# Strassen's second product and another token order for the read-out rows of a fused cross-attention and feed-forward kernel

## The chip, the cores and the metric

The kernel runs on one core of one Trainium2 chip. The metric is the device time of one execution in microseconds. The time before is the median of 13 executions.

## The reference, cut to what matters

There are 8 batches and 8 heads, 512 tokens and 32 state rows for each head, 64 values wide. Attention goes both ways, and the two results are put one behind the other, so that each batch has 512 + 32 = 544 rows of 512 values. A feed-forward stage with exact GELU and d_ff = 2048 follows.

```python
a = softmax(scale * x @ state.T);   xread = a @ state      # 512 rows for each head
a2 = softmax(scale * state @ x.T);  sread = a2 @ x         # 32 rows for each head: the read-out
x = concat([xread, sread], axis=2)  # heads side by side: 8 * 544 rows of 512
h = x @ w_in                        # w_in: 512 x 2048
g = 0.5 * h * (1 + erf(h / sqrt(2)))
out = g @ w_out                     # w_out: 2048 x 512
```

The change concerns the 8 * 32 = 256 read-out rows. Their rows in the output lie at b*544 + 512 to b*544 + 543, for batch b.

## The kernel before, in words

The order of all instructions is written out by hand; each engine takes its instructions in that order. Matrix products have bf16 operands and fp32 sums.

**Token rows.** For a batch, `M` runs the first product in 16 pieces m of 128 hidden values. Each is two matmuls of 512 columns (L478) into a PSUM bank, followed by the GELU on ScalarE (L485), which writes `g`. The second product runs for batches 2 to 7 by Strassen's seven products: `X(b, name)` is one of them, 16 matmuls of 256 columns (L602). VectorE forms the sums of quadrants of `g` that the products need (`g_sum`, L596), sums of quadrants of `w_out` are formed once (`w_sums`), and the products are added up by ScalarE (copies out of PSUM), GpSimd (L621, L650: it forms `v` and `u`) and VectorE (L624, L645, L656, L658).

**Slots.** The last loop goes over batches b = 2 to 7 and eight slots p = 0 to 7. A slot holds two pieces of `M(b)`, one product of batch b - 1 or b, and smaller work. Products 4, 5, 1, 2 and 7 of batch b - 1 run in slots 0 to 4, products 3 and 6 of batch b in slots 6 and 7. Product 2 ends with `c22`: GpSimd forms `v` (L621), then VectorE adds it to the sixth product (L624), then SyncE issues the transfer of half the batch.

**Read-out rows.** `sread` in slot 1 computes a batch's read-out, `sread_out` scales it into `srm`. `srt` transposes `srm` on TensorE (L402), and VectorE copies the result from PSUM to `XSR` (L405), at the columns of that batch, b*32 to b*32 + 31. It stands late in slot 3, after product 2 of the batch before and its `c22`. When `XSR` holds all eight batches, `mm1_sr(m)` runs a piece of the first product for all 256 read-out rows: 4 matmuls of 256 columns (L519) and a GELU of 128x256 (L526) into `g_sr`. Sixteen pieces are needed; four run in each of the slots 4 to 7 of the last batch, between `M` and the product of that slot. The second product, `mm2_sr(s)`, is 16 matmuls of 512 columns for each half s of the rows (L531), a VectorE copy (L539) and an output transfer (L540).

**The end.** After the loop come, for the last batch, the products 4, 5, 1, 2 and 7, with `mm2_sr(0)` after product 4 and `mm2_sr(1)` ahead of product 7. Product 7 is cut in two halves; each ends with a VectorE addition (L678) and a transfer of 128x256 values (L682), the first issued by SyncE, the last by ScalarE.

**Buffers.** Four PSUM banks (the pool `ps_f`) serve the pieces `hp` and `hps`, `srT` and the results of `mm2_sr`. Four more hold the products (`otile`).

Of the kernel before, what the change touches and what calls it, by code (L numbers as in the profile page):

```python
# [9 lines left out]
FP32 = mybir.dt.float32  # L10
BF16 = mybir.dt.bfloat16
AF = mybir.ActivationFunctionType
ALU = mybir.AluOpType
# [4 lines left out]
def kernel(  # L18
# [20 lines left out]
    persist = ctx.enter_context(tc.tile_pool(name="persist", bufs=1))  # L39
    xin = ctx.enter_context(tc.tile_pool(name="xin", bufs=2))  # L40
    att = ctx.enter_context(tc.tile_pool(name="att", bufs=2))
    gpool = ctx.enter_context(tc.tile_pool(name="gpool", bufs=2))
    opool = ctx.enter_context(tc.tile_pool(name="opool", bufs=4))
    hpool = ctx.enter_context(tc.tile_pool(name="hpool", bufs=1))
    apool = ctx.enter_context(tc.tile_pool(name="apool", bufs=3))
    cpool = ctx.enter_context(tc.tile_pool(name="cpool", bufs=1))
    PSUM = bass.MemoryType.PSUM
    ps_f = ctx.enter_context(tc.tile_pool(name="ps_f", bufs=4, space=PSUM))
# [6 lines left out]
    def otile(shape, name, at=None):  # L55
        if at is None:
            at = turn[0] % 4
            turn[0] += 1
        return ps_o.tile(shape, FP32, name=name, tag=f"o{at}")

    def ftile(shape, name):
        return ps_f.tile(shape, FP32, name=name, tag="f")
# [4 lines left out]
    w_out_bf = persist.tile([128, MC, d_model], BF16, name="w_out_bf")  # L67
    ident = persist.tile([128, 128], BF16, name="ident")
    sbd = persist.tile([128, B, HC, 2 * NS], BF16, name="sbd")
    XSR = persist.tile([128, HC, B * NS], BF16, name="XSR")  # L70
    g_sr = persist.tile([128, MC, B * NS], BF16, name="g_sr")
    st_f = persist.tile([128, 2, D], FP32, name="st_f")
    st_bf = persist.tile([128, B, 2, D], BF16, name="st_bf")
# [290 lines left out]
    def atr_dma(b):  # L364
        A = atts[b]
        A.AT = att.tile([128, SJ, 2, 128], BF16, name="AT", tag="AT")
        nc.sync.dma_start_transpose(
            out=A.AT.rearrange("p j t n -> p (j t) n"), in_=A.a
        )
# [29 lines left out]
    def srt(b):  # L399
        A = atts[b]  # L400
        ps = ps_f.tile([128, HC, NS], BF16, name="srT", tag="f")
        nc.tensor.transpose(  # L402
            ps.rearrange("p c n -> p (c n)"), A.srm.rearrange("q t d -> q (t d)"), ident
        )
        nc.vector.tensor_copy(out=XSR[:, :, b * NS:(b + 1) * NS], in_=ps)  # L405

    Ps = {}

# [78 lines left out]
    ops = {}  # L487
# [28 lines left out]
    def mm1_sr(m):  # L516
        hp = ps_f.tile([128, B * NS], FP32, name="hps", tag="f")
        for c in range(HC):
            nc.tensor.matmul(  # L519
                hp,  # L520
                lhsT=w_in_bf[:, c, m * 128:(m + 1) * 128],
                rhs=XSR[:, c, :],
                start=(c == 0),
                stop=(c == HC - 1),
            )
        nc.scalar.activation(out=g_sr[:, m, :], in_=hp, func=AF.Gelu)  # L526

    def mm2_sr(s):
        ps = ps_f.tile([128, d_model], FP32, name="ops", tag="f")
        for m in range(MC):  # L530
            nc.tensor.matmul(  # L531
                ps,
                lhsT=g_sr[:, m, s * 128:(s + 1) * 128],
                rhs=w_out_bf[:, m, :],
                start=(m == 0),
                stop=(m == MC - 1),
            )
        osb = opool.tile([128, d_model], FP32, name="osb", tag="osb")
        nc.vector.tensor_copy(out=osb, in_=ps)  # L539
        nc.sync.dma_start(  # L540
            out=out.rearrange("(b s) n -> b s n", s=SB)[4 * s:4 * s + 4, S:SB, :], in_=osb
        )


    def mm2_m(b, m):
        for j in range(SJ):
# [11 lines left out]
    MH = MC // 2  # L558
    NH = d_model // 2
    w_q = [[w_out_bf[:, MH * k:MH * k + MH, NH * n:NH * n + NH] for n in range(2)] for k in range(2)]  # L560
    w_sum = {}
# [18 lines left out]
        )[i])  # L580

    xs = {}

    def g_q(b, h, k):
        return gs[b][:, MH * k:MH * k + MH, 256 * h:256 * h + 256]

    def g_sum(b, name):
        (h0, k0), (h1, k1), op = {
            "1": ((0, 0), (1, 1), ALU.add),
            "2": ((1, 0), (1, 1), ALU.add),  # L590
            "5": ((0, 0), (0, 1), ALU.add),
            "6": ((1, 0), (0, 0), ALU.subtract),
            "7": ((0, 1), (1, 1), ALU.subtract),
        }[name]
        t = apool.tile([128, MH, 256], BF16, name="gsum", tag="gsum")
        nc.vector.tensor_tensor(out=t, in0=g_q(b, h0, k0), in1=g_q(b, h1, k1), op=op)  # L596
        xs[b, "g" + name] = t
# [13 lines left out]
    def c_tile(name):  # L611
        return cpool.tile([128, 2, NH], FP32, name=name, tag=name)
# [50 lines left out]
    def X1_split(b):  # L663
        xs[b, "q"] = c_tile("q")
        for j in range(2):
            ps = xs[b, "x", j] = otile([128, 1, NH], "xp", 2 - 2 * j)
            x_mm(ps, xs[b, "g1"], w_sum["1"], True, (j,))
            nc.vector.tensor_tensor(
                out=xs[b, "q"][:, j, :], in0=ps[:, 0, :], in1=xs[b, "s34"][:, j, :], op=ALU.add
            )  # L670

    def X7_split(b):
        rows = out[b * SB:b * SB + S, :].rearrange("(p j) n -> p j n", j=SJ)
        o = xs[b, "o", 0]
        for j in range(2):
            ps = xs[b, "x", j]
            x_mm(ps, xs[b, "g7"], w_sum["7"], False, (j,))
            nc.vector.tensor_tensor(  # L678
                out=o[:, j, :NH], in0=ps[:, 0, :], in1=xs[b, "u"][:, j, :], op=ALU.add
            )  # L680
            eng = nc.scalar if j else nc.sync
            eng.dma_start(out=rows[:, j, :NH], in_=o[:, j, :NH])  # L682

    def p_run(b, fs, banks):
        done = []
        for f, at in zip(fs, banks):
            it = iter(at or ())
            tiles = (lambda shape, name: otile(shape, name, next(it))) if at else ftile
            done.append((b, f, p_mm(b, f, tiles)))
        for x in done:  # L690
            p_copy(*x)


    def M(*ms):
        for m in ms:
            mm1(m // MC, m % MC)

    def U(*us):
        for u in us:
            mm2(u // 16, u % 16 // 4, u % 4)  # L700
# [69 lines left out]
    scores(1, 0)  # L770
    scores(1, 1)
    srt(0)
    U(4, 5)
    rearr_ones(1)
# [34 lines left out]
    u = 17  # L809
# [24 lines left out]
    for b in range(2, B):  # L834
        nb = b + 1
        for p in range(8):
            k = 16 * b + 2 * p
            if p == 1 and nb < B:
                scores(nb, 0)
                scores(nb, 1)  # L840
            if p in (2, 3) and nb < B:
                norm(nb, p - 2)
            if p == 3 and nb + 1 < B:
                xtr_dma(nb + 1)
            if p == 5 and nb < B:
                atr_dma(nb)
            M(k, k + 1)
            if nb == B and p >= 4:
                for m in range(4 * p - 16, 4 * p - 12):
                    mm1_sr(m)  # L850
            if b == 2:
                for _ in range(2 if p < 4 else 1):
                    if u < 32:
                        U(u)
                        u += 1
            elif p < 5:
                if p == 0:
                    g_sum(b - 1, "5")
                X(b - 1, "45127"[p])
                if p < 3:  # L860
                    g_sum(b - 1, "127"[p])
            if p == 1:
                sread(b)
                sread_out(b)
            if p == 0 and b + 3 < B:
                nc.gpsimd.tensor_copy(out=hold, in_=gs[b][:, 0, 0:1])  # L866
                load_x(b + 3)
            if p == 0 and nb + 1 < B:
                begin(nb + 1)
                rearr(nb + 1)  # L870
            if p == 2 and nb + 1 < B:
                rearr_ones(nb + 1)
            if p == 3:
                srt(b)
            if p == 5:
                g_sum(b, "6")
                if nb < B:
                    p_run(nb, (0, 1), ((0, 1), (3, 2)))
            if p == 6:
                X(b, "3")  # L880
            if p == 7:
                if nb < B:
                    p_run(nb, (2, 3), ((1, 2), None))
                X(b, "6")
    b = B - 1
    g_sum(b, "5")
    X(b, "4")
    g_sum(b, "1")
    g_sum(b, "2")
    mm2_sr(0)  # L890
    X(b, "5")
    nc.sync.dma_start(
        out=out[b * SB:b * SB + S, :].rearrange("(p j) n -> p j n", j=SJ)[:, 0:2, NH:],
        in_=xs[b, "o", 0][:, :, NH:],
    )
    g_sum(b, "7")
    X1_split(b)
    X(b, "2")
    mm2_sr(1)
    X7_split(b)  # L900


# [28 lines left out]
```

## Time and profile before

| | before |
|---|---|
| median of 13 executions | 216.74 us (215.23 to 219.01) |
| profiled execution, its own time | 216.04 us |
| profiled execution, span | 214.3 us |
| TensorE matmul busy | 201.0 us, 94% of the span |
| VectorE, ScalarE, GpSimd busy | 128.6, 131.2, 65.2 us |
| last matmul group starts | 205.28 us, of 1.91 us |
| last transfer issued | 207.68 us (ScalarE's queue) |

The span runs from the first to the last instruction of one execution that the hardware profiler recorded; the execution's own time holds 1.74 us more, outside that span. Matmuls overlap each other in the array, and their ends are modelled: the distance between starts tells the cost of one, not its listed duration. In the chain of waits each row is a start, a duration and what the end of the program is traced back to in that time; "issue" stands for time in which the engine waited for nothing that the profile shows.

### The profile page before, as it was taken

How to read it: one execution, taken by the hardware profiler on the slowest of the kernel's cores; microseconds unless marked ns; L12 is line 12 of the kernel's file. 1: busy time of each engine (PE TensorE's matmuls, PEld its weight loads, DVE VectorE, ACT ScalarE, POOL GpSimd, SP SyncE). 2: the span in 40 equal slices, each digit the busy share in tenths (PEclk: the TensorE clock that was granted, in tenths of full speed). 3: DMA queues.
4: the chain of work that ended last, by engine and by line, in shares of the span. 5: the costliest groups of instructions: out<-in, count | busy, mean ns of one | idle time of the engine just before them, and what ended most of it. 6: DMA issues, size and time to landing. Idle time of an engine off the chain costs nothing.

```text
span 214.3 us, 4608 instructions
## 1 busy us (share of the span) xinstructions
PE 201.0 (94%) x1939; PEld 128.3 (60%) x1939; DVE 128.6 (60%) x206; ACT 131.2 (61%) x237; POOL 65.2 (30%) x71
## 2 busy tenths in 40 slices
PE   7699999998999999999999999999999969999960
PEld 7445344453444577757774777577757748786740
DVE  2934474739738559955996587558755543026340
ACT  3854765679784877587747784778475445650200
POOL 8955302482370045503572038002200220000400
PEclk9999999999999999999999999999999999999995
DMA  6999999779186709191918700700070002100332
GB/s 200 187 175 204 206 193 172 174 157 185 29 101 145 198 7 165 28 223 26 184 13 258 87 3 2 245 3 2 3 245 0 3 0 123 76 0 3 95 115 85
DMA packets 37837, 23.14 MB, mean 108 GB/s; under 512 B 21688, under 2 KB 35256, under 8 KB 37816
## 3 DMA queue, kind: packets, MB, share of 16 engines
q0 software_dynamic: 13936, 8.10, 27.9%
q1 hardware_dynamic: 23192, 14.29, 27.2%
q10 hardware_dynamic: 688, 0.46, 0.7%
q8 instruction: 15, 0.25, 0.5%
q14 instruction: 6, 0.05, 0.1%
HBM read 17.30 MB, written 8.91 MB: 122 GB/s over the span
## 4 chain that ended last, share of the span: by engine, by line
PE 83%; DMA 7%; ACT 3%; issue 1%; POOL 1%; DVE 1%; SPq 0%; ACTq 0%
PE xp L602 34%; PE hp L478 24%; PE op L504 9%; DMA w_out_bf<-in_moe_w_out_dram 6%; PE p_ps L415 4%; PE hps L519 3%; PE ops L531 3%; DMA x0f<-in_x_dram 2%; PE op L549 2%; PE pt L324 1%; PE sr L378 1%; ACT g L485 1%; ACT L485 1%; ACT L331 1%; POOL v L621 1%
## 5 line engine op out<-in xcount | busy, mean ns | idle before, releaser
L485 ACT ACTIVATE g<-hp 128x512 bf16<-128x512 f32 x124 | 67.5, 603 | 32.2 <-PE hp L478 27.4
L478 PE MATMUL hp<-AT,P 128*128 128x512 bf16 x248 | 63.9, 380 | 0.1
L602 PEld LDWEIGHTS <-gsum 128*128 128x128 bf16 x480 | 46.5, 98 | 11.9 <-issue 2.1
L596 DVE TENSOR_TENSOR gsum<-g 128x2048 bf16<-128x2048 bf16 x30 | 39.8, 1342 | 7.9 <-ACT g L485 6.8
L602 PE MATMUL xp<-ws,gsum 128*128 128x256 bf16 x288 | 34.4, 273 | 0.0
L478 PEld LDWEIGHTS <-P 128*128 128x128 bf16 x248 | 22.2, 98 | 20.4 <-issue 2.9
L427 DVE CAST P<-p_ps 128x512 bf16<-128x512 f32 x31 | 20.0, 683 | 18.4 <-PE p_ps L415 18.4
L650 POOL TENSOR_TENSOR u<-s,oh 128x512 f32<-128x512 f32 x6 | 8.0, 1332 | 69.9 <-ACT oh L648 69.9
L504 PE MATMUL op<-w_out_bf,g 128*128 128x512 bf16 x96 | 23.7, 379 | 0.4 <-DMA w_out_bf<-in_moe_w_out_dram 0.4
L602 PE MATMUL xp<-w_out_bf,gsum 128*128 128x256 bf16 x192 | 22.9, 273 | 0.0
L602 PE MATMUL xp<-ws,g 128*128 128x256 bf16 x192 | 22.9, 273 | 0.0
L426 ACT CAST P<-p_ps 128x512 bf16<-128x512 f32 x31 | 17.0, 604 | 7.3 <-PE p_ps L415 7.3
L602 PEld LDWEIGHTS <-g 128*128 128x128 bf16 x192 | 18.8, 98 | 4.3
L504 PEld LDWEIGHTS <-g 128*128 128x128 bf16 x96 | 9.1, 98 | 12.0 <-issue 1.6
L218 POOL COPY x<-xb 128x1024 bf16<-128x1024 bf16 x12 | 12.6, 1083 | 11.4 <-DMA xb<-in_x_dram 11.4
L228 POOL COPY xo<-xb 128x1024 bf16<-128x1024 bf16 x12 | 14.6, 1244 | 1.3 <-PE sr L378 1.3
L347 DVE TENSOR_TENSOR a<-e,ics 128x512 bf16<-128x512 bf16 x14 | 13.8, 986 | 0.5
L645 DVE TENSOR_TENSOR s<-xp,s 128x512 f32<-128x512 f32 x6 | 4.2, 692 | 14.2 <-PE xp L602 14.2
L621 POOL TENSOR_TENSOR v<-q,oh 128x512 f32<-128x512 f32 x6 | 7.7, 1283 | 13.4 <-ACT oh L652 13.4
L415 PE MATMUL p_ps<-w_in_bf,sbd 64*32 64x512 bf16 x248 | 11.2, 382 | 0.6 <-ACT g L485 0.5
L344 DVE TENSOR_REDUCE cs<-e 128x16 f32<-128x512 bf16 x14 | 9.5, 676 | 3.8 <-ACT e L331 3.8
L866 POOL COPY hold<-g 128x1 bf16<-128x1 bf16 x3 | 1.0, 332 | 31.1 <-ACT g L485 31.1
(91 smaller groups left out, 201.5 us busy)
## 6 DMA issues: line engine op xcount, KB each, us to landing
out_dram<-oh SPq DMA_DIRECT2D x11, 512.0 KB, 3.3
xb<-in_x_dram POOLq DMA_DIRECT2D x7, 512.0 KB, 6.8
out_dram<-osb SPq DMA_DIRECT2D x9, 256.0 KB, 3.6
w_out_bf<-in_moe_w_out_dram POOLq DMA_DIRECT2D x4, 512.0 KB, 13.2
w_in_bf<-in_moe_w_in_dram POOLq DMA_DIRECT2D x6, 256.0 KB, 12.1
x0f<-in_x_dram SPq DMA_DIRECT2D x3, 256.0 KB, 3.5
w_in_bf<-in_moe_w_in_dram POOLq DMA_DIRECT2D x4, 128.0 KB, 4.1
x0f<-in_x_dram ACTq DMA_DIRECT2D x1, 256.0 KB, 4.2
```

The source lines that it names most:

```text
L218: nc.gpsimd.tensor_copy(out=A.x4[:, :, :, 64 * t:64 * t + 64].rearrange("p j c d -> p c j d"), in_=src[:, t],)
L228: eng.tensor_copy(out=A.xo[:, :, :, 2 + 64 * t:66 + 64 * t].rearrange("p j c d -> p c j d"), in_=src[:, t],)
L347: nc.vector.tensor_tensor(out=A.a[:, :, hs].rearrange("p g (c n) -> p g c n", n=NS), in0=e4, in1=ics[:, :, :].to_broadcast((128, G, 2, NS) ...
L415: nc.tensor.matmul(ps[t][32 * c:32 * c + 32, :], lhsT=sbd[64 * t:64 * t + 64, b, c, 32 * t:32 * t + 32], rhs=w_in_bf[64 * t:64 * t + 64, c ...
L426: nc.scalar.copy(out=dst[:, 0, :], in_=ps[0])
L427: nc.vector.tensor_copy(out=dst[:, 1, :], in_=ps[1])
L478: nc.tensor.matmul(hp, lhsT=Ps[b][:, t, m * 128:(m + 1) * 128], rhs=atts[b].AT[:, :, t, :], start=(t == 0), stop=(t == 1),)
L485: nc.scalar.activation(out=gs[b][:, m, :], in_=hp, func=AF.Gelu)
L504: nc.tensor.matmul(ps, lhsT=gs[b][:, m, j * 128:(j + 1) * 128], rhs=w_out_bf[:, m, :], start=(m == 0), stop=(m == MC - 1),)
L596: nc.vector.tensor_tensor(out=t, in0=g_q(b, h0, k0), in1=g_q(b, h1, k1), op=op)
L602: nc.tensor.matmul(ps[:, j - js[0], :], lhsT=lhs[:, m, 128 * j:128 * j + 128], rhs=rhs[:, m, :], start=(first and j == js[0] and m == 0), ...
L621: nc.gpsimd.tensor_tensor(out=xs[b, "v"], in0=xs[b, "q"], in1=o[:, :, :NH], op=ALU.subtract)
```

## The change

There are four edits.

1. `XSR` has its columns in the order state row, batch, where before they were in the order batch, state row. VectorE's copy in `srt` then writes every eighth element. All products on the read-out rows have their rows in that order, and a transfer of 128 rows covers 16 state rows of 8 batches.
2. `srt(b)` stands at the start of slot 3, ahead of `M` and of product 2 of the batch before with its `c22`, for all b from 2 to 7.
3. The pieces `mm1_sr` run in slots 3 to 6 of the last batch, after the slot's product where it has one, and not in slots 4 to 7 ahead of it.
4. `mm2_sr` is gone. In its place stand `r_sums`, five sums of quadrants of `g_sr` of 128x1024 on VectorE, and seven products `R(name)` of 8 matmuls of 256 columns, with their additions on ScalarE, VectorE and GpSimd. They are put between the products of the last batch. The sums of `w_out` are those already there. Each half of the rows is written by one transfer, `r_out`, both near the end.

The sums use buffers of `xT` and `AT`, whose readers have finished by then. The diff, cut:

```diff
-    XSR = persist.tile([128, HC, B * NS], BF16, name="XSR")
+    XSR = persist.tile([128, HC, NS, B], BF16, name="XSR")
...
-        nc.vector.tensor_copy(out=XSR[:, :, b * NS:(b + 1) * NS], in_=ps)
+        nc.vector.tensor_copy(out=XSR[:, :, :, b], in_=ps)
...
-                rhs=XSR[:, c, :],
+                rhs=XSR[:, c, :, :].rearrange("p n b -> p (n b)"),
...
-    def mm2_sr(s):
...
-        nc.sync.dma_start(
-            out=out.rearrange("(b s) n -> b s n", s=SB)[4 * s:4 * s + 4, S:SB, :], in_=osb
-        )
...
+    def r_q(h, k):
+        return g_sr[:, MH * k:MH * k + MH, 128 * h:128 * h + 128]
+
+    def r_sums():
+        pair = [att.tile([128, 2, MH, 128], BF16, name="rs", tag="xT") for _ in range(2)]
+        one = att.tile([128, MH, 128], BF16, name="rs1", tag="AT")
+        homes = [pair[0][:, 0], pair[0][:, 1], pair[1][:, 0], pair[1][:, 1], one]
+        for name, t in zip("51267", homes):
+            (h0, k0), (h1, k1), op = G_SUMS[name]
+            nc.vector.tensor_tensor(out=t, in0=r_q(h0, k0), in1=r_q(h1, k1), op=op)
+            rs["g" + name] = t
+
+    def r_out(h):
+        nc.sync.dma_start(
+            out=out.rearrange("(b s) n -> s b n", s=SB)[S + 16 * h:S + 16 * h + 16],
+            in_=rs["o", h],
+        )
+
+    def R(name):
...
+        for m in range(MH):
+            nc.tensor.matmul(
+                ps,
+                lhsT=lhs[:, m, :],
+                rhs=rhs[:, m, :],
+                start=(first and m == 0),
+                stop=(m == MH - 1),
...
+        if name == "3":
+            nc.scalar.copy(out=c_new("s3"), in_=ps)
...
+        elif name == "4":
+            nc.vector.tensor_tensor(out=c_new("s34"), in0=ps, in1=rs["s3"], op=add)
+        elif name == "5":
+            o = rs["o", 0][:, NH:]
+            nc.scalar.copy(out=o, in_=ps)
+            nc.gpsimd.tensor_tensor(out=c_new("u"), in0=rs["s34"], in1=o, op=sub)
+        elif name == "1":
+            nc.vector.tensor_tensor(out=c_new("q"), in0=ps, in1=rs["s34"], op=add)
+        elif name == "2":
+            o = rs["o", 1][:, :NH]
+            nc.scalar.copy(out=o, in_=ps)
+            nc.gpsimd.tensor_tensor(out=c_new("v"), in0=rs["q"], in1=o, op=sub)
+        elif name == "6":
+            nc.vector.tensor_tensor(out=rs["o", 1][:, NH:], in0=ps, in1=rs["v"], op=add)
+            r_out(1)
+        elif name == "7":
+            nc.vector.tensor_tensor(out=rs["o", 0][:, :NH], in0=ps, in1=rs["u"], op=add)
+            r_out(0)
...
+            if p == 3:
+                srt(b)
             M(k, k + 1)
-            if nb == B and p >= 4:
-                for m in range(4 * p - 16, 4 * p - 12):
-                    mm1_sr(m)
...
+            if nb == B and 3 <= p < 7:
+                for m in range(4 * p - 12, 4 * p - 8):
+                    mm1_sr(m)
...
-            if p == 3:
-                srt(b)
...
     b = B - 1
+    r_sums()
     g_sum(b, "5")
     X(b, "4")
     g_sum(b, "1")
+    R("3")
+    R("4")
     g_sum(b, "2")
-    mm2_sr(0)
     X(b, "5")
...
+    R("5")
+    X1_split(b)
     g_sum(b, "7")
-    X1_split(b)
+    R("1")
     X(b, "2")
-    mm2_sr(1)
+    R("2")
+    R("6")
+    R("7")
     X7_split(b)
```

More of the change, by code (lines that the diff above doesn't have):

```diff
@@ L526, in mm1_sr @@
         nc.scalar.activation(out=g_sr[:, m, :], in_=hp, func=AF.Gelu)
-    def mm2_sr(s):
[L529 to L536, printed above, removed]
-            )
-        osb = opool.tile([128, d_model], FP32, name="osb", tag="osb")
-        nc.vector.tensor_copy(out=osb, in_=ps)
-        nc.sync.dma_start(
-            out=out.rearrange("(b s) n -> b s n", s=SB)[4 * s:4 * s + 4, S:SB, :], in_=osb
-        )
     def mm2_m(b, m):
@@ L582 @@
     xs = {}
+    G_SUMS = {
+        "1": ((0, 0), (1, 1), ALU.add),
+        "2": ((1, 0), (1, 1), ALU.add),
+        "5": ((0, 0), (0, 1), ALU.add),
+        "6": ((1, 0), (0, 0), ALU.subtract),
+        "7": ((0, 1), (1, 1), ALU.subtract),
+    }
     def g_q(b, h, k):
@@ L587, in g_sum @@
     def g_sum(b, name):
[L588 to L594, printed above, removed]
+        (h0, k0), (h1, k1), op = G_SUMS[name]
         t = apool.tile([128, MH, 256], BF16, name="gsum", tag="gsum")
@@ L682, in X7_split @@
             eng.dma_start(out=rows[:, j, :NH], in_=o[:, j, :NH])
+    rs = {}
+    def r_q(h, k):
[5 more added lines that the diff above has]
+        for name, t in zip("51267", homes):
+            (h0, k0), (h1, k1), op = G_SUMS[name]
+            nc.vector.tensor_tensor(out=t, in0=r_q(h0, k0), in1=r_q(h1, k1), op=op)
+            rs["g" + name] = t
@@ new lines, in r_out, with c_new @@
+    def r_out(h):
[4 more added lines that the diff above has]
+    def R(name):
+        def c_new(n):
+            rs[n] = cpool.tile([128, NH], FP32, name="r_" + n, tag="r_" + n)
+            return rs[n]
+        bank = {"3": 0, "4": 1, "5": 0, "2": 1, "1": 2, "6": 3, "7": 2}[name]
+        first = name in "3416"
+        if first:
+            rs[bank] = ftile([128, NH], "rp")
+        ps = rs[bank]
+        lhs = {"3": (0, 0), "4": (1, 1)}.get(name)
+        lhs = rs["g" + name] if lhs is None else r_q(*lhs)
+        rhs = {"5": w_q[1][1], "2": w_q[0][0]}.get(name)
+        rhs = w_sum[name] if rhs is None else rhs
+        for m in range(MH):
[5 more added lines that the diff above has]
+                stop=(m == MH - 1),
+                skip_group_check=True,
+            )
+        add, sub = ALU.add, ALU.subtract
+        if name == "3":
+            nc.scalar.copy(out=c_new("s3"), in_=ps)
+            for h in range(2):
+                rs["o", h] = opool.tile([128, d_model], FP32, name="osb", tag="osb")
+        elif name == "4":
[16 more added lines that the diff above has]
+            r_out(0)
```

## The prediction

> **What bounds the kernel now.** I read the page's first part, then the chain of waits over the last 45 us, then the waits by engine, and last the busy time in stretches behind the last matmul. TensorE is busy for 94% of the span, so only three things can shorten it: fewer matmul columns, a hole in TensorE's row, or a shorter end behind the last matmul. The chain:
>
> ```profile
> PE 201.0 (94%) x1939; PEld 128.3 (60%) x1939; DVE 128.6 (60%) x206; ACT 131.2 (61%) x237; POOL 65.2 (30%) x71
> ```
> ```profile
> 171.03 0.86 PE hp L478 x4
> 171.89 0.69 PE xp L602 x7
> 172.58 1.14 issue
> 173.72 0.59 ACT oh L652
> 174.31 0.07 issue
> 174.38 1.27 POOL v L621
> 175.68 0.04 DVE oh L624
> 175.71 0.57 issue
> 176.28 0.23 DVE XSR L405
> 176.51 0.05 issue
> 176.55 1.92 PE hps L519 x16
> ...
> 189.80 3.49 PE xp L602 x32
> 193.29 3.45 PE ops L531 x16
> 196.75 5.25 PE xp L602 x48
> 201.99 3.45 PE ops L531 x16
> 205.44 1.76 PE xp L602 x16
> 207.23 0.42 DVE oh L678
> ```
> ```profile
> PE hps L519 <- DVE XSR L405: 2.0, 1, 2.0
> ```
>
> The chain leaves TensorE from 172.58 to 176.55: ScalarE, GpSimd and VectorE finish `c22`, and only then does VectorE copy the transposed read-out (L405), for which the first `mm1_sr` waits. The pieces of `M` started at 173.53 and cost 0.86, so TensorE could have gone on at 174.39: the hole is 176.55 - 174.39 = **2.16 us** (the waits list 2.0). From 176.55 to 207.2 TensorE has no hole. `mm2_sr` is 3.45 twice.
>
> Behind the last matmul stands the output:
>
> ```profile
> 205.50:207.00 1.50, 1.50 (x16) 1.27 (x13) 1.10 (x2) 0.00 (x0) 0.00 (x0) 1.00 0.85 350
> 207.00:209.00 2.00, 0.19 (x2) 0.00 (x0) 0.42 (x1) 0.00 (x0) 0.00 (x0) 1.00 0.37 46
> 209.00:210.50 1.50, 0.00 (x0) 0.00 (x0) 0.00 (x0) 0.00 (x0) 0.00 (x0) 0.58 0.67 199
> 210.50:212.00 1.50, 0.00 (x0) 0.00 (x0) 0.00 (x0) 0.00 (x0) 0.00 (x0) 0.50 0.25 88
> ```
> ```profile
> out_dram<-oh SPq DMA_DIRECT2D x1, 128.0 KB, 5.3
> out_dram<-oh ACTq DMA_DIRECT2D x1, 128.0 KB, 4.8
> ```
>
> The last columns are the DMA share and GB/s. The 512 KB of L616, issued at 204.79, move at 350 GB/s. From 210.5 to 212.0 the share is 0.25: four of sixteen engines still move bytes, at 88 GB/s. These are the second half of the read-out (L540, issued at 206.20). The last transfers, 128 KB each, were issued at 206.86 and 207.68 and land 5.3 and 4.8 later, the last at 212.5; the remaining 1.8 to 214.3 is the program's end.
>
> **What the Trainium skill says.** "DMA: Bandwidth & Descriptors", section "Why a DMA increments its semaphore by 16 and not by 1": the transfer takes the largest number of engines up to 16 that divides the slowest dimension on both sides. Before, the read-out's output side has 4 (batches), so 4 engines; after, 16. The 0.25 agrees. "TensorE: Matmul & The Clock Gate", section "Back-to-back issue gap", gives 262 cycles for 256 columns and 518 for 512, at 2.4 GHz 109 and 216 ns; the chain has 1.75/16 = 109 and 3.45/16 = 216, so it agrees. "VectorE: DVE Perf Modes", section "The perf-mode tier table", gives 1224 ns for a bf16 sum of 2048; the trace has 1220 (L596).
>
> **The change, part by part.** The durations are of the profiled execution: span 214.3, own time 216.04, 0.70 under the median of 216.74. I work out what the end moves by and take that from the median.
>
> *1. `srt` one step sooner, `mm1_sr` behind the slot's product.* `srm` is ready at 168.88; slot 3 starts on TensorE at 170.85. The transposes cost 0.06 either way. VectorE has L656 and L596 ahead, done at 172.9, so `XSR` is ready near 173.1, ahead of `c22`. TensorE: transpose, `M` to 171.77, product 2 to 173.52, then `mm1_sr` at once. Slots 3 to 6 hold 0.86 + 1.75 + 1.75 (no product in slot 5), slot 7 holds `M` and product 6: **product 4 starts at 189.22, before at 191.38: -2.16.** What is late next? The hidden pieces need GELUs: ScalarE has 1.08 + 4 x 0.40 + 0.59 = 3.3 in a slot of 4.36, and the banks follow it. Slot 5 has 2.7 in 2.61; before, the same two pieces of work followed each other there without a hole (`mm1_sr` from 180.92, the next `M` from 182.67).
>
> In batches 2 to 6 the transposes move sooner too, and TensorE would stand still if `srm` were late. It is ready at 62.6, 83.8, 105.5, 126.5 and 147.9; slot 3 starts near 64.5, 85.0, 106.7, 128.4 and 150.0, so 1.1 is the least room. L405 comes after the norm and ahead of L624 on VectorE; together they take as long. Its strided write is not shown: 0.21 at best; doubled, it would delay p_ps (which waits for L658) by 0.2 in batches 3 and 4, where VectorE is full. I take 0 and keep +0.5. SyncE's queue is not passed: L616 of the first half may leave 0.13 later, with 512 KB landing in 3.3 and nobody waiting.
>
> *2. Seven products for two halves.* Away: 2 x 3.45 = 6.90. Added: 7 x 8 x 0.1094 = 6.12. **-0.78.** The weight loads (98 ns) lie under matmuls of 109, as in `X`. Nothing on TensorE may wait, so I put the clocks beside each other. `r_sums` needs the last `g_sr`: TensorE ends it at 184.85, ScalarE at 185.5. Five sums of half of L596's size: two in a row take 2.35 (L596 at 193.94), so about 0.6 each; and by the cycles of the VectorE page (section "Side-by-side: where the cycles go for N=2048 bf16": half the elements plus 158, at 0.96 GHz) 0.70, an estimate. That is 3.0 to 3.5, done by 189.0. The last token GELU ends at 188.5, so `g_sum` 5 is ready at 190.2 and product 5 wants it at 192.71. Sum 1 is ready at about 193.1, wanted at 195.34. Sum 2 is ready at 194.6, wanted at 197.96. The bank of the second half of product 1 comes free at 195.25 (ScalarE's copy, 0.59), wanted at 196.21: **0.96, the tightest.** `g_sum` 7 is done at 198.9, wanted at 202.34. `R` 7 waits for q at 199.2, wanted at 201.46. So TensorE runs 189.22 + 5 x 1.75 + 6.12 = 204.09.
>
> *3. Additions.* VectorE loses two copies of 0.69 and gets five sums and four adds of 0.42; ScalarE gets three copies under 0.59; GpSimd two differences, about half of 1.27. At the end: product 2 leaves TensorE at 199.71, ScalarE's copy ends at 200.5, `v` at 201.8, L624's add at 202.55; GpSimd's second difference ends at 202.45, `R` 6's add at 203.0, `R` 7's at 203.4. Product 7's first half is ready at 203.4 and its second at 204.3, so they are not queued: done at 204.7. If GpSimd took 1.65 (as L650 once does), 0.4 would still fit. Without that cover, each 0.4 would count once.
>
> *4. The transfers.* SyncE issues 512 KB at 202.6, then two of 256 KB at 203.0 and 203.5 (0.56 each, as L540), then 128 KB at 204.2; ScalarE's last leaves at 204.75, before at 207.68: -2.93, which is parts 1 and 2. Before, half of the read-out had left at 197.50; now both halves are at the end. 1.28 MB at 350 GB/s from 203.4 take 3.7, to 207.1, and L616 landed 0.4 after its bytes: 207.5. From the other side: L616 at its fastest took 2.6 from issue to landing, which would be 207.35 for the last 128 KB, and 4.8 if nothing gets better, 209.55. I take 207.6; the bounds are 207.1 and 209.55. **-4.9 against 212.5**, of which 2.0 is the tail.
>
> Sum: -2.16 - 0.78 - 2.0 = -4.9. Profiled: 216.04 - 4.9 = 211.1, span 209.4. Median: 216.74 - 4.9 = **211.8**.
>
> **Rivals.** *A, the tail stays.* The slow stretch at 207 to 209 (46 GB/s while the share is 0.37) may not be the four engines' doing, and 256 KB more are in it now, in rows of 2 KB that lie 544 rows apart. Then the last transfer lands 4.8 after its issue and only parts 1 and 2 count: 216.74 - 2.93 = 213.8. For it: L892 alone, at 199.18, also took 5.0. Against it: it too followed an L540. Chance 0.2.
>
> *B, a new wait eats the hole.* The transposes at the head of slot 3 hold TensorE in all six batches if VectorE is late with `srm`; a delay of 1.1 plus 0.7 in two batches, or a bank in the last slots, gives back 1.5 to 3: about 214.2. Against it: the rooms above. Chance 0.06.
>
> *C, slower.* If the new transfer were spread over few engines (22 GB/s each, 88/4), both halves would sit ahead of the last 128 KB. On 4 engines 512 KB take 6.0 from 203.4: landing near 210. From 2 engines on it decides: 11.9, landing at 216 and later, 3.5 behind 212.5: 220.3. The share of 0.25 with 4 rows speaks against it. Chance 0.04. That Strassen's form does not shorten TensorE can be excluded only as far as the columns set the pace; that is so for `X`.
>
> **How the numbers follow.** My forecast has 0.7. About 0.5% (1.1 us) is what a measurement of this kernel can tell from no change. A is beyond it; of B's 0.06, spread about its middle, 0.02 lie beyond it, 0.03 within and 0.01 on the slower side. Faster 0.7 + 0.2 + 0.02 = 0.92; same 0.03; slower 0.04 + 0.01 = 0.05. The range runs from the tail's best, 216.74 - 5.4, less 0.5 for the scatter of a median, to A with 0.4 above: 210.8 to 214.2.
>
> **What would show it.** `mm1_sr` starts at about 173.5 with no wait for L405; product 4 near 189.2; the last matmul near 204; five sums near 0.65; share no longer 0.25 behind the last matmul, and the last transfers landing in about 3. I am wrong if TensorE shows holes in slot 3 or among the `R`, or if the last transfers still take 5.

## The result and the profile after

The kernel after takes 212.54 us (median of 11 executions, 211.77 to 213.08). The kernel before, timed beside it and in all earlier runs, takes 217.1 us (48 executions, 214.96 to 219.01). The ratio is 0.9801, with a 95% interval of 0.9774 to 0.9829: 4.3 us less by the ratio, 4.6 by the medians. The forecast was 211.8, with a range of 210.8 to 214.2. In the profiled execution the own time is 212.02 against 216.04, and the span 210.3 against 214.3. Times without a unit are us throughout.

Read the first part and the chain first:

```profile
PE 201.4 (96%) x1963; PEld 131.1 (62%) x1963; DVE 135.4 (64%) x213; ACT 132.9 (63%) x240; POOL 66.4 (32%) x73
```

The chain of waits of the kernel after, from slot 3 of the last batch to the end (start, duration, what):

```profile
171.75 0.86 PE hp L478 x4
172.62 1.75 PE xp L586 x16
174.37 1.81 PE hps L519 x16
176.18 0.86 PE hp L478 x4
...
188.36 3.49 PE xp L586 x32
191.86 1.75 PE rp L703 x16
193.60 1.75 PE xp L586 x16
195.35 0.87 PE rp L703 x8
196.22 1.75 PE xp L586 x16
197.97 0.87 PE rp L703 x8
198.84 1.75 PE xp L586 x16
200.59 2.62 PE rp L703 x24
203.21 1.76 PE xp L586 x16
...
205.00 0.42 DVE oh L662
```

From slot 3 of the last batch on, the chain stays on TensorE until the last matmul. The first `mm1_sr` (L519) follows product 2 (L586, L602 before) at once. The seven `R` (L703) cost 1.75 + 0.87 + 0.87 + 2.62 = 6.11, and no row lies between them and the products. What TensorE does wait for from batch 2 on is in the waits by engine, and these two lines were not in the profile before:

```profile
PE hp L478 <- DVE XSR L405: 0.4, 2, 0.2
PE hp L478 <- DMA AT<-a: 0.3, 1, 0.3
```

Next, the instructions behind them, by tile. Columns: shortest, median and longest duration in ns, then first and last start. First the kernel before, then the kernel after:

```profile
L405 DVE COPY XSR<-srT x8: 208/214/226, 21.9 to 176.3; 128x128 bf16<-128x128 bf16 x8
```
```profile
L405 DVE COPY XSR<-srT x8: 715/726/734, 21.6 to 173.5; 128x128 bf16<-128x128 bf16 x8
L679 DVE TENSOR_TENSOR rs<-g_sr x5: 684/686/693, 186.2 to 188.6; 128x1024 bf16<-128x1024 bf16 x5
```

The copy of the read-out costs 3.4 times as much as before. The sums of `r_sums` cost 0.686 each; the timeline has the five in one row of 3.10 from 186.21.

The busy time in stretches at the end, after (last three columns: granted clock, which is the share of TensorE's full speed that it was granted, DMA share, GB/s), and the last transfers (median from issue to landing):

```profile
204.00:205.50 1.50, 0.96 (x9) 0.61 (x7) 0.93 (x3) 0.00 (x0) 0.00 (x0) 1.00 0.88 355
205.50:206.50 1.00, 0.00 (x0) 0.00 (x0) 0.00 (x0) 0.00 (x0) 0.00 (x0) 1.00 0.96 246
206.50:208.00 1.50, 0.00 (x0) 0.00 (x0) 0.00 (x0) 0.00 (x0) 0.00 (x0) 0.91 0.98 352
208.00:210.30 2.30, 0.00 (x0) 0.00 (x0) 0.00 (x0) 0.00 (x0) 0.00 (x0) 0.50 0.02 5
```
```profile
out_dram<-oh SPq DMA_DIRECT2D x1, 128.0 KB, 3.0
out_dram<-oh ACTq DMA_DIRECT2D x1, 128.0 KB, 3.0
```

The DMA engines stay at a share of 0.88 to 0.98 until the bytes are gone; the stretch at 0.25 has disappeared. The last transfer leaves at 205.45 and lands at 208.46, 4.0 sooner than before.

**The balance of the two profiles.** I laid the start of the same pieces of `M` beside each other, after minus before. The profile after enters the batches 0.78 ahead, by its start and its loads. It loses 0.48 in batch 3 and 0.48 in batch 4 behind L405, and 0.48 in batch 5 at `AT<-a`; the rest up to the last batch is 0.07. Then -2.16 (the hole) and -0.79 (6.90 to 6.11). That is -0.78 + 1.51 - 2.16 - 0.79 = -2.2 at TensorE's end (207.2 to 204.97), and -1.8 in the last transfer (4.8 to 3.0): -4.0, the own times' difference.

Where a batch loses its 0.48 is seen in the timeline of the kernel after, batch 3, slot 3:

```profile
89.56 0.71 DVE L405 COPY XSR<-srT 128x128 bf16<-128x128 bf16 x1
89.90 0.90 DVE L608 TENSOR_TENSOR oh<-xp,v 128x512 f32<-128x512 f32 x1
90.33 0.59 PE L478 MATMUL hp<-AT,P 128*128 128x512 bf16 x2 [0.17 <-DVE XSR L405]
...
90.71 0.68 DVE L642 TENSOR_TENSOR oh<-xp,u 128x512 f32<-128x512 f32 x1
...
90.85 0.99 PE L415 MATMUL p_ps<-w_in_bf,sbd 64*32 64x512 bf16 x16
```

`srT` takes one of the four banks of `hp`; it comes free only when L405 ends, at 90.27, and `M` waits 0.17 for it; its second piece starts 0.77 behind the first, where before it was 0.43. Behind L405, VectorE adds `c22` (L608) and then L642, whose bank is needed by `p_ps` (L415, a product that goes into `P`): L415 starts behind `M` but takes 0.99, where before it took 0.84 at this place and 0.62 elsewhere.

### The profile page after: what moved, and what is told of

It reads as the page before. It is cut to its first block, busy times and chain, and to the rows that moved or that the text cites. A ratio compares the mean times of both kernels' runs of the same rounds, so it can differ in the third digit from the quotient of the medians.

```text
span 210.3 us, 4674 instructions
## 1 busy us (share of the span) xinstructions
PE 201.4 (96%) x1963; PEld 131.1 (62%) x1963; DVE 135.4 (64%) x213; ACT 132.9 (63%) x240; POOL 66.4 (32%) x73
## 4 chain that ended last, share of the span: by engine, by line
PE 75%; DVE 11%; POOL 4%; DMA 3%; ACT 2%; issue 1%; POOLq 0%; DVEq 0%; ACTq 0%
PE xp L586 27%; PE hp L478 21%; PE op L504 9%; DVE gsum L580 5%; PE p_ps L415 4%; PE op L532 3%; PE hps L519 3%; DMA AT<-a 3%; PE rp L703 3%; DVE a L347 2%; POOL w_in_bf L105 2%; DVE cs L344 1%; PE sr L378 1%; PE pt L324 1%; POOL sbd L95 1%
## 5 line engine op out<-in xcount | busy, mean ns | idle before, releaser
L586 PEld LDWEIGHTS <-gsum 128*128 128x128 bf16 x480 | 46.6, 98 | 11.9 <-issue 2.1
L586 PE MATMUL xp<-ws,gsum 128*128 128x256 bf16 x288 | 34.4, 273 | 0.0
L586 PE MATMUL xp<-ws,g 128*128 128x256 bf16 x192 | 22.9, 273 | 0.0
L586 PE MATMUL xp<-w_out_bf,gsum 128*128 128x256 bf16 x192 | 22.9, 273 | 0.0
L586 PEld LDWEIGHTS <-g 128*128 128x128 bf16 x192 | 18.8, 98 | 4.3
L415 PE MATMUL p_ps<-w_in_bf,sbd 64*32 64x512 bf16 x248 | 11.1, 382 | 0.6 <-ACT g L485 0.5
```

The costliest lines, as they stand in the source:

```text
L415: nc.tensor.matmul(ps[t][32 * c:32 * c + 32, :], lhsT=sbd[64 * t:64 * t + 64, b, c, 32 * t:32 * t + 32], rhs=w_in_bf[64 * t:64 * t + 64, c ...
L586: nc.tensor.matmul(ps[:, j - js[0], :], lhsT=lhs[:, m, 128 * j:128 * j + 128], rhs=rhs[:, m, :], start=(first and j == js[0] and m == 0), ...
```

## The experiments

Ratios are to the kernel before on the same chip, with 95% intervals. "Edit 1" to "edit 4" are those of the change.

### The order of the tokens alone

The kernel before with edit 1; `mm2_sr` keeps its place.

```diff
-    XSR = persist.tile([128, HC, B * NS], BF16, name="XSR")
+    XSR = persist.tile([128, HC, NS, B], BF16, name="XSR")
-        nc.vector.tensor_copy(out=XSR[:, :, b * NS:(b + 1) * NS], in_=ps)
+        nc.vector.tensor_copy(out=XSR[:, :, :, b], in_=ps)
-            out=out.rearrange("(b s) n -> b s n", s=SB)[4 * s:4 * s + 4, S:SB, :], in_=osb
+            out=out.rearrange("(b s) n -> s b n", s=SB)[S + 16 * s:S + 16 * s + 16], in_=osb
```

> The kernel before with the first edit alone: the columns of XSR in the order state row, batch, and each half of the read-out written by a transfer with 16 outermost rows; slots, moves and second product as before. Theory (four engines held up the end; the strided copy L405 costs on VectorE): the last transfer lands about 3.0 after its issue instead of 4.8, -1.8; the copy takes 0.72 instead of 0.21, which is on the chain in the last batch's hole (+0.5) and delays the p_ps of batches 3 and 4 (+0.5 each): about -0.3 in sum, 0.998 of before. Rival (the end got short for another reason, as the Strassen form or the later transfers): the last transfer still takes 4.8, and the kernel is about 1.5 slower, 1.007.

216.14 us, ratio 0.9977 (0.9952 to 1.0003): the number fits, though the terms are larger on both sides. The tail does shorten: the last two transfers take 2.2 and 2.6, not 4.8 and 5.3. But TensorE loses 0.43, 0.43, 0.37 and 0.26 in batches 3 to 6, where `p_ps` waits for L658 behind the longer copy, and the hole in slot 3 grows by L405's extra time. Its waits by engine, and stretches from the hole on (first PE and its count; third column from the end: granted clock):

```profile
PE hps L519 <- DVE XSR L405: 2.5, 1, 2.5
```
```profile
175.40:178.70 3.30, 1.03 (x10) 0.93 (x11) 1.32 (x2) 0.89 (x3) 0.86 (x1) 1.00 0.26 106
178.80:182.10 3.30, 3.30 (x18) 2.38 (x16) 0.00 (x0) 1.11 (x3) 0.00 (x0) 0.50 0.11 42
182.20:186.00 3.80, 3.80 (x30) 2.83 (x29) 1.82 (x2) 2.42 (x6) 0.00 (x0) 1.00 0.34 137
```

A second effect was not expected: behind the hole the granted clock is 0.50 for 3.4 us. The next two groups of 16 matmuls take 2.59 and 2.74 in the chain, where behind the hole of the kernel before they took 1.92 and 1.75: 1.7 more, which is half of 3.4. The last section works out when the clock fell.

### The moves alone

The kernel before with edits 2 and 3; order, copy and `mm2_sr` as before.

```diff
+            if p == 3:
+                srt(b)
             M(k, k + 1)
-            if nb == B and p >= 4:
-                for m in range(4 * p - 16, 4 * p - 12):
...
+            if nb == B and 3 <= p < 7:
+                for m in range(4 * p - 12, 4 * p - 8):
                     mm1_sr(m)
...
-            if p == 3:
-                srt(b)
```

> The kernel before with the second and third edit alone: the transposes at the head of slot 3, and the pieces of the first read-out product in slots 3 to 6 behind the slot's product. Theory: the hole of 2.16 in the last batch goes and nothing else changes, since L405 keeps its 0.21: -2.2, 0.990. Rival (the transposes at the head of the slot are themselves what costs TensorE 0.5 in batches 3 and 4): -1.2, 0.9945, with waits of hp for L405 in the trace.

214.32 us, ratio 0.9891 (0.9849 to 0.9933): -2.4 us by the ratio, near the hole's 2.16. In the profile TensorE ends 1.5 sooner: 2.17 for the hole, less 0.48 lost in batch 5, where `M` waits for `AT<-a` here too, and less 0.17 of the start and of batches 3 and 4. TensorE has no wait for L405 in any batch, so the rival falls: the early place alone does not cost the 0.48 of batches 3 and 4. The tail is untouched (4.8, 5.3).

### Moves and Strassen in the old order

The kernel after without edit 1.

```diff
-    XSR = persist.tile([128, HC, NS, B], BF16, name="XSR")
+    XSR = persist.tile([128, HC, B * NS], BF16, name="XSR")
...
-            out=out.rearrange("(b s) n -> s b n", s=SB)[S + 16 * h:S + 16 * h + 16],
+            out=out.rearrange("(b s) n -> b s n", s=SB)[4 * h:4 * h + 4, S:SB, :],
```

> The changed kernel without the first edit: columns of XSR in the order batch, state row again, and each half of the read-out written by a transfer with 4 outermost rows. Theory: TensorE gains the hole and the fewer columns (-2.9) with no loss in batches 3 and 4, but both halves now go at the end over the same four engines at 22 GB/s each, 512 KB in 6.0, so that the end lands near 210.4 to 211 in the clock of the profile before: -1.5 to -2.1 in all, 0.990 to 0.993. Rival (the number of engines of the transfer does not matter): -2.9 - 1.8, 0.978 or better, faster than the changed kernel.

216.89 us, ratio 1.003 (1.0007 to 1.0052): no better than the kernel before, and far from what the theory and the rival gave. TensorE is not at fault. The chain ends its matmuls at 204.46, sooner than in the kernel after. The end of the profile tells the rest, in the stretches and the transfers:

```profile
203.50:205.00 1.50, 0.94 (x9) 0.59 (x7) 0.91 (x3) 0.00 (x0) 0.00 (x0) 1.00 0.86 350
205.00:207.00 2.00, 0.00 (x0) 0.00 (x0) 0.00 (x0) 0.00 (x0) 0.00 (x0) 1.00 0.25 19
207.00:209.00 2.00, 0.00 (x0) 0.00 (x0) 0.00 (x0) 0.00 (x0) 0.00 (x0) 0.92 0.71 181
209.00:212.50 3.50, 0.00 (x0) 0.00 (x0) 0.00 (x0) 0.00 (x0) 0.00 (x0) 0.50 0.27 101
```
```profile
out_dram<-oh SPq DMA_DIRECT2D x1, 128.0 KB, 8.7
out_dram<-oh ACTq DMA_DIRECT2D x1, 128.0 KB, 7.4
```

A share of 0.25 is four of the sixteen engines. For 2 us they are busy and move 19 GB/s; later, at a share of 0.27, 101 GB/s are moved. Four engines thus finish two transfers of 256 KB late, and the two small ones, issued behind them, land 7.4 and 8.7 after their issue. The products that gain 0.78 put both halves at the end, and in the old order that costs as much as hole and products give: the moves alone had 0.9891. So edit 4 needs edit 1, or another way to spread the transfers over more engines. The theory took the four engines at the 22 GB/s each of the profile before and had no slow start, which is a part of what it missed.

### The order made by the matmul's reading

The kernel after, with `XSR` in the old order and the reordering in the moving operand, read in steps of 32 elements (64 bytes).

```diff
-                rhs=XSR[:, c, :, :].rearrange("p n b -> p (n b)"),
+                rhs=XSR[:, c, :].rearrange("p (b n) -> p n b", b=B),
```

> The changed kernel, but VectorE writes XSR in the order batch, state row (a write without steps), and the matmuls of mm1_sr read their moving operand with a step of 32 elements, so that the rows come out in the order state row, batch all the same. Theory (the strided write of L405 cost the changed kernel about 1.0 to 1.5 in batches 3 and 4): L405 takes 0.21 again, TensorE shows no wait for it, and if the matmul does not mind the step the kernel takes 1.0 to 1.5 less than the changed one, 0.974 to 0.976 of before. Rival (the step costs TensorE instead): the 64 matmuls L519 take longer than 109 ns from start to start, at double the time 7 more, 1.01 of before. Rival (the 0.7 by which TensorE was late was no matter of L405): no change against the changed kernel, 0.980.

236.51 us, ratio 1.0939 (1.0885 to 1.0994). The theory that the step is free on this side falls, and the first rival's direction holds, with a larger size. By tile, and a stretch with the last of these matmuls (third column from the end: granted clock):

```profile
L519 PE MATMUL hps<-XSR,w_in_bf x64: 590/607/613, 173.2 to 207.3; 128*128 128x256 bf16 x64
L405 DVE COPY XSR<-srT x8: 209/218/226, 21.5 to 172.5; 128x128 bf16<-128x128 bf16 x8
```
```profile
195.90:212.80 16.90, 16.90 (x48) 6.42 (x47) 3.10 (x5) 5.07 (x11) 0.00 (x0) 0.50 0.00 0
```

In the kernel after, L519 has 273 ns; here 607. In the chain, 16 of them take 6.86 to 6.88, 0.43 each from start to start instead of 0.109: the array is fed at about a quarter of the pace. That costs 20 us (four times 5.1). Another 5 are the clock: it falls to 0.50 three times while L519 runs, and the pieces of `M` and products between take twice their time (1.71 for 0.86, 3.42 for 1.75). Less the 1.0 that batches 3 and 4 no longer lose, these are the 24 over the kernel after. L519 itself keeps its 0.43 at 1.00 (the first twelve) and at 0.50 (the last sixteen), so its pace is not that of TensorE's clock. L405 is short again, and with it the wait for L405 is gone from all batches, so that wait is the strided write's doing.

### The kernel after without Strassen's products

Edits 1 to 3, with `mm2_sr` at its old places and one transfer of 16 outermost rows for each half.

```diff
-    r_sums()
...
-    R("3")
-    R("4")
     g_sum(b, "2")
+    mm2_sr(0)
...
-    R("2")
-    R("6")
-    R("7")
+    mm2_sr(1)
```

> The changed kernel without the fourth edit: mm2_sr stands where it stood before, after product 4 and ahead of product 7, 16 matmuls of 512 columns each, with the transfer of 16 outermost rows. Theory (Strassen's form gains 0.78 on TensorE, but sends both halves at the end, where 512 KB more than the last 768 KB go out in one queue): TensorE ends 0.8 later, the last transfer lands 2.2 to 2.4 after its issue instead of 3.0, so that nearly all of the 0.78 is back: within 0.3 of the changed kernel, 0.979 to 0.982 of before. Rival (the transfers at the end cost nothing): 0.8 slower than the changed kernel, 0.984.

212.69 us, ratio 0.9828 (0.9776 to 0.9879), which can't be told from the kernel after. One half leaves early here, the last two transfers take 2.2 and 2.6, and TensorE has 0.78 more. Strassen's form gains 0.78 on TensorE and gives up to 0.8 back in the last transfer (3.0 against 2.2).

### The order made by the GELU

The kernel after with `XSR` in the old order; the GELU reads PSUM in steps of 32 values and writes `g_sr` in the new order.

```diff
-        nc.scalar.activation(out=g_sr[:, m, :], in_=hp, func=AF.Gelu)
+        nc.scalar.activation(
+            out=g_sr[:, m, :].rearrange("p (n b) -> p n b", b=B),
+            in_=hp.rearrange("p (b n) -> p n b", b=B),
+            func=AF.Gelu,
+        )
```

> The changed kernel, but XSR stays in the order batch, state row (short write on VectorE, plain reads on TensorE), and the GELU of mm1_sr reads PSUM with a step of 32 values and writes g_sr in the order state row, batch. Theory (ScalarE does not mind the step in PSUM): L405 0.21, the GELUs of 128x256 about 0.4 as before, batches 3 and 4 lose no 0.48 each: 0.7 to 1.2 under the changed kernel, 0.975 to 0.977 of before. Rival (ScalarE pays as TensorE did, 2 or 3 times the time): the GELUs take 0.8 to 1.1, ScalarE becomes the bound in slots 3 to 6 with about 5.5 in slots of 4.4 and 2.6, and the kernel is 3 to 6 slower than the changed one.

211.15 us, ratio 0.9753 (0.9705 to 0.9801). By tile:

```profile
L526 ACT ACTIVATE g_sr<-hps x16: 383/383/392, 174.7 to 185.5; 128x256 bf16<-128x256 f32 x16
```

The GELU takes 0.383 with the step and 0.384 without it (the run above and the kernel after, same tile). L405 is back at 0.218, and TensorE has no wait for it; the wait for `AT<-a` stays. The gain over the kernel after, 0.9801 - 0.9753 = 0.5% or 1.0 us, fits the 0.96 that batches 3 and 4 lost; the trace shows them gone, but the intervals of the two ratios overlap.

### The old order with more transfers

The kernel after in the old order, each half in four transfers of one batch, one half by ScalarE's queue and one by SyncE's.

```diff
+        for i in range(4):
+            eng = nc.sync if h else nc.scalar
+            eng.dma_start(
+                out=out.rearrange("(b s) n -> b s n", s=SB)[4 * h + i, S:SB, :],
+                in_=rs["o", h][32 * i:32 * i + 32, :],
+            )
```

> The changed kernel with the old order of columns (L405 short) and each half of the read-out written by four transfers of 32 rows, one for each batch, the first half's by ScalarE's queue, the second's by SyncE's. Theory (what matters is that the slowest dimension has 16 or 32, not the order of tokens): no loss at L405, the transfers use all sixteen engines, and the last one lands about 3.0 after its issue; eight issues of about 0.35 cost the end 0 to 0.7: 0.3 to 1.2 under the changed kernel, 0.975 to 0.979 of before. Rival (each small transfer has its own fixed time on the engines, or the issues hold up the last two): slower than the changed kernel by 1 or more, 0.985.

211.25 us, ratio 0.9755 (0.971 to 0.9801). The transfers by size:

```profile
out_dram<-osb SPq DMA_DIRECT2D x4, 64.0 KB, 2.5
out_dram<-osb ACTq DMA_DIRECT2D x4, 64.0 KB, 2.5
out_dram<-oh SPq DMA_DIRECT2D x1, 128.0 KB, 2.3
out_dram<-oh ACTq DMA_DIRECT2D x1, 128.0 KB, 2.4
```

The same bytes to the same rows land in 2.5 when the outermost count is 32 and not 4. So where the rows lie does not make the long tail: the doubt that rival A rested on is settled. This run also has smaller transfers on two queues; the kernel with the order alone has whole 256 KB transfers on one queue, and its last ones land in 2.2 and 2.6. What the two share is the outermost count. The last issue here is only at 206.51 (the four of SyncE's queue take 2.59), and the median, 211.25, is that of the order made by the GELU (211.15).

### The transposes late again, but for the last batch

```diff
-            if p == 3:
+            if p == 3 and nb == B:
                 srt(b)
             M(k, k + 1)
...
+            if p == 3 and nb < B:
+                srt(b)
```

> The changed kernel with the second edit undone in batches 2 to 6: srt stands late in slot 3 there, behind product 2 of the batch before, and at the head of slot 3 only in the last batch. Theory (the long L405 costs where L642 waits behind it): as in the kernel with the order alone, batches 3 to 6 lose about 0.43, 0.43, 0.37 and 0.26, together 1.5, where the changed kernel lost 0.96 in batches 3 and 4: 0.5 slower than the changed kernel, 0.9825 of before. Rival (the early place is what made L405 cost): no loss, 1.0 faster than the changed kernel, 0.9755.

212.46 us, ratio 0.9815 (0.9769 to 0.9861): no difference to the kernel after that can be measured. The trace says why: it loses 1.49 behind L405, as the order alone did, and nothing at `AT<-a`; the kernel after loses 1.45 at both together.

### Three versions on the reordering GELU

The first adds the late transposes of the run before. The second changes the order at the end, so that the products on the read-out rows come before the last of the token rows:

```diff
+    g_sum(b, "2")
     R("3")
-    R("4")
-    g_sum(b, "2")
     X(b, "5")
...
-    R("5")
+    R("4")
     X1_split(b)
     g_sum(b, "7")
+    X(b, "2")
+    R("5")
     R("1")
-    X(b, "2")
     R("2")
```

(then `R` 6, 7 and the two halves of product 7, as before). The third does both.

> The kernel with the order turned in the GELU's read (short L405), and srt late in slot 3 in batches 2 to 6, early in the last one. In every trace with the early srt TensorE waited 0.3 for the transfer AT<-a in batch 5 and lost 0.48 there; in the three traces with the late one it did not. Theory (the early place brings the two output transfers of c22 nearer to the transposing transfer): no wait for AT, 0.5 under the kernel with the turned GELU, 0.973 of before. Rival (the wait for AT comes and goes by chance, or comes from the changed end of the batch before): the wait is there, no change, 0.975.

> The kernel with the order turned in the GELU's read, and another order of products at the end: X4, R3, X5, R4, X1, X2, then R5, R1, R2, R6, R7, then X7. The 512 KB of c22 then leave some 1.8 sooner, and 768 KB are left for the end where there were 1.28 MB. Theory (the end lasts as long as the bytes in flight with the last transfer): the last transfer lands 2.2 to 2.4 after its issue instead of 3.0, with TensorE as before: 0.6 to 0.8 under the kernel with the turned GELU, 0.972 of before. Rival (R7 waits for q, which stands behind c22's addition on VectorE with 0.25 of room): TensorE loses 0.3 to 0.8 there and nothing is gained, 0.975.

> Both edits of the two kernels beside it: the late srt in batches 2 to 6 and the other order of products at the end. Theory: they add up, 1.1 to 1.3 under the kernel with the turned GELU, 0.970 of before. Rival: one of the two has no effect, 0.9725.

They take 210.74 (ratio 0.9703, 0.9667 to 0.9738), 210.70 (0.9699, 0.966 to 0.9737) and 210.46 us (0.9683, 0.9648 to 0.9718). The first loses nothing in the batches. In the second, the last transfers take 2.3 and 2.6 after their issue, and the chain still has no hole:

```profile
194.00 3.49 PE xp L590 x32
197.49 4.37 PE rp L707 x40
201.86 1.76 PE xp L590 x16
```

The third is the best version that ran: 3.2% below the kernel before, and 1.2% below the kernel after. Among the three, differences lie inside the intervals. In the third the wait for `AT<-a` came back in part (0.36 lost), though its transposes are late: the theory that late transposes always remove that wait falls.

### The kernel before once more

> The kernel before, unchanged, profiled once more. In the profile of the kernel with the order alone TensorE's granted clock fell to 0.64 for some 5 behind a hole of 2.7, and the matmuls there took 1.7 more; in the profile before the hole was 2.16 and the clock stayed at 1. The times before spread over 4, those of the changed kernel, without a hole, over 1.3. Theory: the hole before is near the length at which the clock falls, so that some executions before pay 1 to 2 behind it: a hole of 2.2 and a clock of 0.6 to 0.8 in the 5 behind it, if this execution is among them. Rival: the clock stays at 1 behind a hole of 2.2, and the spread is of the start (first product of batch 0 between 17.2 and 19.6 in the profiles so far).

One more execution, profiled to see whether the clock also falls behind the hole of the kernel before: 215.78 us, and it did not. The stretch behind the hole has a granted clock of 1.00:

```profile
176.50:180.00 3.50, 3.50 (x34) 3.03 (x31) 0.02 (x1) 1.53 (x4) 0.00 (x0) 1.00 0.37 150
```

Its transposing transfer took up to 6.2 to land, and `M` of batch 5 waited for it here too (0.41 lost). Over the fourteen profiles of this case, the wait is there where the slowest `AT<-a` that the trace lists takes 6.1 or more from issue to landing (6.3 after) and absent at 5.8 and less (5.6 in the first profile of before). With the transposes early it is there in eight of eight, with them late in two of six. So it doesn't need the early transposes; that they make it likelier (edit 2) is suggested by these counts, and what delays that transfer is open.

## Why the prediction was right, and where its sum was not

**The hole, -2.16: right.** `mm1_sr` follows product 2 without a wait, and the moves alone took 2.17 from TensorE's row at this place. The absolute starts (174.37 for 173.5, 189.95 for 189.22) are late by what batches 3 to 5 lost, less the earlier start.

**L405's strided write: the mis-sized term.** I had it at 0.21, or doubled, took 0 and kept 0.5. It takes 0.726, not 0.42, and costs 0.48 in batch 3 and 0.48 in batch 4. The place was right, VectorE's queue in front of L624 (L608 after) and L658 (L642 after), with `p_ps` behind it. But I named one waiter of two: `srT`'s bank is the second, and `M` asks for it. That the write is the cause is shown by the five runs that keep `XSR` contiguous with the transposes in the early place: none waits for L405.

**Strassen's products, -0.78: right on TensorE.** 6.11 for 6.12, no wait among the `R`. The five sums were 3.0 to 3.5 in the sum and 3.10 on the chip; each is 0.686, close to the 0.70 that I had estimated from the Trainium skill, "VectorE: DVE Perf Modes", section "Side-by-side: where the cycles go for N=2048 bf16". As a part of the whole the products bring nothing that could be measured: in the run without them TensorE has 0.78 more, and the last transfer lands 0.8 sooner after its issue, with one half gone early. Step 4 had both halves at the end in its 2.85, so the sum holds; it did not ask what the end would take without them.

**The transfers, -2.0 in the tail: right in size and in cause.** Measured -1.8: 3.0 after the issue, not the 2.85 (204.75 to 207.6) of the sum. The order alone brought the last transfer from 4.8 to 2.2. What the Trainium skill says in "DMA: Bandwidth & Descriptors", section "Why a DMA increments its semaphore by 16 and not by 1", carried this step, and the runs agree: share 0.25 with 4 outermost rows, 0.96 with 16, and 64 KB in 2.5 with 32. One reading was short: the bytes at a share of 0.25 before were not all the read-out's. The packets of 2 KB, its rows, end near 211.5; among them and after them, up to 212.1, come packets of 1 KB, the rows of the last two transfers. The last issue came at 205.45, 0.7 after my 204.75, which is again what the batches lost.

**The rivals.** A, the tail stays, is refuted: it fell from 4.8 to 3.0. B took something back, but not by its mechanism; `srm` was in time everywhere, and what waited was the bank and `p_ps` behind a longer copy. C, few engines, is refuted by the share. The price of few engines was shown by the run in the old order, with four of them: 216.89.

**What the median holds beside the sum.** The profiles' -4.0 holds +0.96 (L405) and +0.48 (`AT<-a`) that I had not, and -0.78 of an earlier start that belongs to no edit. That the profile's -4.0 comes close to the sum's -4.9 is in part luck: the early start hides half of what was lost. With the 0.96 in it the sum would have been -3.9. A part of the medians' difference may be the clock, as the last section says.

## What to carry to other kernels

A reordering is not free because its count of elements is unchanged: try it on each side that touches the data, and price it there. Here VectorE's write cost 0.5 more for each copy, the matmul that read with the step took four times as long, and ScalarE's read of PSUM cost nothing. Look at the outermost count of every output transfer near the end, since one with few rows there also held back those behind it; and when work is moved to the end to save TensorE a little, count the bytes that now leave there.

## What the runs showed of the hardware that I had not expected

- **A bf16 write with a step is dear on VectorE.** A copy of 128x128 from PSUM took 0.726 when it wrote every eighth element (16 bytes apart), and 0.214 when it wrote contiguously.
- **A moving operand read in steps of 64 bytes fed the array at about a quarter of the pace:** 0.43 us for 256 columns, against 0.109, and the same 0.43 at a granted clock of 1.00 and of 0.50.
- **Transfers on four engines began slowly:** in the kernel with the old order, 2 us at 19 GB/s before 101 GB/s. This was read from one profile.
- **A hole in TensorE's work can cost more than itself, by where it falls.** The clock records of the fourteen traces hold only 1.00 and 0.50, and the clock changes only at the ends of steps of 3.41 us, counted from its first rise. I counted TensorE's idle time in each step that ran at 1.00. Wherever it was 1.47 or less, the next step had 1.00 again, but for three steps of the reading with steps of 64 bytes, which have no idle time; wherever it was 1.65 or more, the next had 0.50. The hole of 2.7 in the kernel with the order alone put 2.33 into one step, and the next ran at 0.50 and cost 1.7. The hole of 2.2 in the kernel before put 1.45 into one step in the first profile and 1.29 in the second, and nothing followed. By these counts the same hole costs 1.7 more where one step holds it whole; no profile of the kernel before caught that.
- **The mean clocks of the executions fit this, without showing it.** The kernel with the order alone has a median of 216.3 in the 11 executions with a mean clock below 0.990, and 215.26 in the 11 others. The kernel before, over 66 executions, has 217.66 in the 18 at 0.981 to 0.983 and 216.09 in the 48 others; both of its profiles (0.988 and 0.990) are of the larger group. The kernel after, which has no such hole, has none below 0.993. If the 18 are those with a step at 0.50, some 0.5 of the gain in the median (216.6 over these 66 against 216.09) goes with the clock. A mean alone doesn't tell, since it also holds the half clock behind the last matmul: the kernel with the old order has no hole and lies at 0.975 to 0.987.
